# A fused attention and mixing kernel: casting loads gated by the third V block in place of the fourth, and another order of its 761 steps

## The chip, the cores and the metric

The kernel runs on one core of one Trainium2 chip. The metric is the device time of one execution in microseconds (us). A core has five engines that take their instructions from queues of their own and meet only at semaphores: PE (TensorE, matrix multiplication and transposes), DVE (VectorE), ACT (ScalarE, exponentials and sines), POOL (GpSimd, which also issues the DMAs that convert float32 to bfloat16) and SP (SyncE, which here issues all other DMAs). PEld in the profile is the loading of weights into PE, beside its matmuls.

## The reference

Four sequences of 768 positions go through an attention of 8 heads of 64 columns and then through a mixing layer. Heads 0, 2 and 6 are causal over all positions; the other five see the first 4 positions and a window of 64.

```python
scores = (1/8) * q @ k.T                      # per batch and head, 768 x 768
a = softmax(where(mask[head], scores, -1e9))
x = concat_heads(a @ v)                       # (4, 768, 512)
theta = x @ w_theta
zr, zi = x * cos(theta), x * sin(theta)
y = einsum('ts,bsd->btd', w_tok_r, zr) + einsum('ts,bsd->btd', w_tok_i, zi)
u = x + y
out = u + maximum(u @ w_ch, 0)                # float32
```

Inputs and output are float32; products are computed in bfloat16.

## The kernel before

**Tiles.** Each batch is cut into 6 blocks of 128 positions. The heads go in pairs, (0,2), (4,6), (1,3), (5,7), numbered 0 to 3. Scores are computed transposed and only where the mask leaves something: 17 units per batch, numbered 0 to 16. Units 0, 1, 2, 10, 11 and 12 belong to head pair 0; 3, 4, 5, 13 and 14 to pair 1; 6, 7 and 15 to pair 2; 8, 9 and 16 to pair 3. The eight PSUM banks are named in the steps, singly or as pairs starting at 0, 2, 4 and 6.

**Order.** Nothing is scheduled by a program. `ORDER` (line 57) is a list of 761 steps; the loop at line 535 runs them in turn, and each appends its instructions to the queue of its engine. A step is a name, its indices, a PSUM bank where it needs one, and at the end, for copies and elementwise products, the engine: A, D or P for ACT, DVE or POOL. Dependences become semaphore waits, so within one engine the list's order is the order of execution, and a waiting step holds all behind it on that engine.

**Steps.** In the order in which a batch b meets them:

- `k` constants (line 191): i the identity, a memsets on DVE, s four selects on POOL, b the masks' copies and negations on DVE, c other memsets. `kv` empties `vo` (line 215). `w.n` is n warm-up matmuls.
- `lf` (line 223): q and k of head pairs 0 and 1 of batch 0, as float32 on SP's queue, 384 KB each; `cf` (line 271) converts them on an engine. `lq` (line 228): the other q and k loads, converted by the DMA, on POOL's queue.
- `lv` (line 233): V in 6 blocks of 256 KB, float32, on SP's queue, into `st_v`. `cv` (line 388) converts a block into `vt`; `bv` copies part of it into `vo` for the window's previous block, `sv` the first four rows.
- `tq`, `eq` (lines 252, 267): transposes of q or k on PE and the copy out of PSUM (`ea`, `eb` in two parts). `ko` (line 276): the keys of the window's previous block with the first four.
- `pm`, `s`, `e`, `m`: in batch 0 masks are added in PSUM by `pm`; scores, exponentials, and in later batches a mask by DVE after the exponential.
- `av`, `n`: values of one block of rows and division by their sum, which gives x. `xp` with `xe` transposes x through PE (batch 0), `xd` by a DMA transpose on SP (line 421).
- `th`, `tr`, `z`: theta for two blocks, ACT's cosine and sine of it, and the products zr (part r) and zi (part i). `mx.b.t.p` (line 464): 4 matmuls of row block t with two of the six columns blocks of w_tok_r and w_tok_i; three such make y. `u` adds x. `ud` transposes u on SP, `up` with `ue` through PE. `ch`, `o`, `st`: product with w_ch, the final sum, the store. `ci`, `oi`, `si` are halves of these.
- `lw`, `lt`: the weights, converted by DMAs on POOL's queue; `wt`, `we` transpose w_tok through PE.

**Gates.** Two steps exist to hold loads back. `gw` (line 240) copies one element of a V block of batch 0 to a scrap tile on POOL, which therefore waits until that block has landed; the weights' loads `lw.t` and `lt` stand behind it on POOL's queue. `gv` (line 236) makes the V loads of batch 1 wait for a w_tok load.

```python
HOLD_V, HOLD_W = (5, 0), 3
...
    def hold_w():

        nc.gpsimd.tensor_copy(scrap, st_v[:1, HOLD_W, 0, :1])
```

Of the kernel before, what the change touches and what calls it, by code (L numbers as in the profile page):

```python
# [50 lines left out]
HOLD_V, HOLD_W = (5, 0), 3  # L51
# [6 lines left out]
k.i lf.q.0 k.a lf.k.0 lq.0.q.2 w.11.7 lf.q.1 kv.0.D lq.0.k.2 lf.k.1 k.s lv.0.0 w.11.7 lv.0.1 k.c cf.q.0.A lv.0.2 w.5.7 lq.0.q.3 k.b tq.0.q.0.0  # L58
lq.0.k.3 w.9.7 cf.k.0.A eq.0.q.0.0.A tq.0.k.0.1 pm.0.0.2 pm.0.12.4 ea.0.k.0.1.A pm.0.1.6 eb.0.k.0.1.A s.0.0.2 e.0.0.2 s.0.12.4 cf.q.1.P s.0.1.6
pm.0.2.0 lv.0.3 e.0.12.4 tq.0.q.2.2 e.0.1.6 cf.k.1.D s.0.10.4 tq.0.q.1.3 e.0.10.4 tq.0.k.1.6 eq.0.q.1.3.D s.0.2.0 eq.0.k.1.6.A eq.0.q.2.2.D s.0.11.4  # L60
lv.0.4 tq.0.k.2.3 e.0.2.0 ko.0.1.P pm.0.4.6 eq.0.k.2.3.D e.0.11.4 pm.0.3.0 cv.0.0.P s.0.4.6 s.0.3.0 bv.0.0.D e.0.4.6 s.0.14.2 ko.0.2.D pm.0.6.4
# [50 lines left out]
def kernel(ctx: ExitStack, tc: tile.TileContext, q, k, v, is_retrieval, n_sink, window, w_theta, w_tok_r, w_tok_i, w_ch, out):  # L112
    nc = tc.nc
# [119 lines left out]
    def load_v(b, j):  # L233
        nc.sync.dma_start(out=st_v[:, j], in_=v[b, :, j * 128:(j + 1) * 128].rearrange("h p d -> p h d"))
# [338 lines left out]
```

## Time and profile before

| | |
|---|---|
| median of 4 runs | 180.02 us (178.49 to 180.79) |
| the profiled execution | 179.5 us, of which 177.8 from its first to its last instruction |
| PE busy | 165.8 us (93%), 1793 matmuls in the record |
| PEld busy | 94.9 us (53%) |
| DVE busy | 138.5 us (78%) |
| ACT busy | 112.0 us (63%) |
| POOL busy | 54.7 us (31%) |
| granted PE clock | 1.00 |

The share of busy time is an average over stages. In a row of slices each digit is the busy share of a fortieth of the span in tenths. A timeline row has the start, the time that the instruction or run of instructions took, the engine (SPq is SP's queue of issues), the line, what is written and read, the count, and in brackets how long the engine stood idle before and what ended that. Matmuls overlap in their pipeline, so PE's busy time overstates its load; the distance from one start to the next is the better measure. The profile's own "x" counts miss a few matmuls; the weight loads, one ahead of each matmul, are complete, and times of PE steps are read from these.

### The profile page before, as it was taken

The numbers are of one execution on the slowest core, as the hardware profiler recorded it, in microseconds if no ns is written. First come the engines' busy times: TensorE is split into PE (matmuls) and PEld (weight loads), VectorE is DVE, ScalarE is ACT, GpSimd is POOL, SyncE is SP. The second block draws the span as 40 slices with busy tenths as digits, with TensorE's granted clock in tenths as the row PEclk, the third lists the DMA queues.
The fourth block names the chain that finished last, engine by engine and source line by source line (L and its number), as shares of the span: only waits on it lengthen the run. The fifth ranks groups of instructions, "written<-read, shape, count | busy, mean of one in ns | idle before, by whom it ended". The sixth has DMA issues, their size and how long they took to land.

```text
span 177.8 us, 4412 instructions
## 1 busy us (share of the span) xinstructions
PE 165.8 (93%) x1793; PEld 94.9 (53%) x1819; DVE 138.5 (78%) x268; ACT 112.0 (63%) x132; POOL 54.7 (31%) x86
## 2 busy tenths in 40 slices
PE   6868999999999998998999999999999999998992
PEld 6635578656654684543546864444445654443441
DVE  6347878898978977999869898979997928970483
ACT  3889999998999316798975408998761274300000
POOL 8414585686008800789160020040010000200000
PEclk9999999999999999999999999999999999999999
DMA  5997899999899999599999594957514548007856
GB/s 175 225 217 166 146 194 200 201 207 195 153 195 204 171 135 152 84 237 237 218 251 144 123 120 100 162 157 236 151 30 118 88 91 267 0 0 111 214 164 224
DMA packets 62372, 28.73 MB, mean 162 GB/s; under 512 B 48400, under 2 KB 59408, under 8 KB 62352
## 3 DMA queue, kind: packets, MB, share of 16 engines
q1 hardware_dynamic: 51952, 19.54, 53.9%
q0 software_dynamic: 10400, 8.92, 33.7%
q8 instruction: 14, 0.23, 0.6%
q14 instruction: 6, 0.05, 0.1%
HBM read 25.69 MB, written 6.29 MB: 180 GB/s over the span
## 4 chain that ended last, share of the span: by engine, by line
PE 70%; DMA 16%; DVE 7%; SPq 2%; issue 2%; POOL 0%; DVEq 0%
PE big L467 30%; PE big L450 9%; PE big L480 8%; PE big L323 8%; DMA st_v<-in_v_dram 7%; PE big L410 7%; DMA early<-early 4%; PE big L259 4%; DVE early L462 3%; DVE ot L483 2%; DMA uT<-u 2%; PE big L441 2%; DMA out_dram<-ot 2%; PE big L298 1%; SPq L226 1%
## 5 line engine op out<-in xcount | busy, mean ns | idle before, releaser
L353 ACT ACTIVATE P<-big 128x1024 bf16<-128x1024 f32 (+2 forms) x64 | 56.9, 947 | 11.3 <-PE big L323 11.1
L467 PE MATMUL big<-early,wtokTi 128*128 128x512 bf16 x71 | 26.9, 379 | 0.6 <-issue 0.5
L467 PE MATMUL big<-zi,wtokTi 128*128 128x512 bf16 x69 | 26.1, 379 | 0.6 <-issue 0.5
L467 PE MATMUL big<-early,wtokTr 128*128 128x512 bf16 x67 | 25.4, 380 | 0.1
L467 PE MATMUL big<-zr,wtokTr 128*128 128x512 bf16 x66 | 25.1, 380 | 0.3 <-DVE ot L483 0.2
L480 PE MATMUL big<-w_ch_sb,uT 128*128 128x512 bf16 (+1 forms) x96 | 23.7, 371 | 0.9 <-DMA uT<-u 0.7
L483 DVE SCALAR_TENSOR_TENSOR ot<-big,u 128x512 f32<-128x512 f32 (+1 forms) x25 | 16.3, 663 | 8.6 <-PE big L480 7.5
L467 PEld LDWEIGHTS <-wtokTr 128*128 128x128 bf16 x144 | 14.0, 98 | 16.5 <-issue 1.6
L467 PEld LDWEIGHTS <-wtokTi 128*128 128x128 bf16 x144 | 14.1, 98 | 14.1 <-issue 0.5
L323 PE MATMUL big<-qT,kT 64*128 64x128 bf16 (+3 forms) x240 | 19.4, 247 | 0.4 <-DVE ot L483 0.3
L410 PEld LDWEIGHTS <-P 128*128 128x128 bf16 x472 | 16.7, 97 | 3.8 <-DVE P L367 0.2
L410 PE MATMUL big<-vt,P 128*128 128x65 bf16 x372 | 17.2, 193 | 0.1
L454 ACT ACTIVATE ct<-big,half_pi 128x1024 f32<-128x1024 f32 x12 | 13.4, 1118 | 5.7 <-PE big L450 4.9
L375 DVE TENSOR_TENSOR P<-P,m_stream 128x1024 bf16<-128x1024 bf16 (+3 forms) x27 | 15.1, 569 | 2.2 <-ACT P L353 2.1
L480 PEld LDWEIGHTS <-uT 128*128 128x128 bf16 x100 | 9.1, 98 | 11.2 <-DMA uT<-u 1.4
L323 PEld LDWEIGHTS <-kT 64*128 64x128 bf16 x240 | 10.6, 94 | 7.4 <-issue 5.1
L265 POOL COPY kO<-kT 64x320 bf16<-64x320 bf16 (+3 forms) x10 | 4.4, 464 | 26.9 <-PE big L410 12.8
L462 POOL TENSOR_TENSOR early<-early,st 128x512 bf16<-128x512 bf16 x4 | 5.7, 1429 | 22.4 <-ACT st L455 22.4
L455 ACT ACTIVATE st<-big 128x1024 f32<-128x1024 f32 x12 | 12.3, 1022 | 0.0
L265 DVE COPY qT<-big 128x768 bf16<-128x768 bf16 x12 | 11.2, 948 | 1.0 <-PE big L259 1.0
L450 PE MATMUL big<-w_theta_sb,early 128*128 128x512 bf16 x45 | 10.9, 379 | 0.9 <-DMA early<-early 0.8
L263 ACT COPY kT<-big 128x768 bf16<-128x768 bf16 (+2 forms) x7 | 4.9, 713 | 10.5 <-PE big L259 9.3
(89 smaller groups left out, 286.4 us busy)
## 6 DMA issues: line engine op xcount, KB each, us to landing
st_v<-in_v_dram SPq DMA_DIRECT2D x24, 256.0 KB, 4.6
out_dram<-ot SPq DMA_DIRECT2D x23, 256.0 KB, 2.4
qb<-in_q_dram POOLq DMA_DIRECT2D x14, 192.0 KB, 6.8
kb<-in_k_dram POOLq DMA_DIRECT2D x14, 192.0 KB, 7.4
wtok<-in_moe_w_tok_r_dram POOLq DMA_DIRECT2D x6, 192.0 KB, 6.9
wtok<-in_moe_w_tok_i_dram POOLq DMA_DIRECT2D x6, 192.0 KB, 7.1
early<-in_q_dram SPq DMA_DIRECT2D x2, 384.0 KB, 5.4
early<-in_k_dram SPq DMA_DIRECT2D x2, 384.0 KB, 6.4
```

What stands on the lines that cost most here:

```text
L265: (nc.vector if eng == "D" else nc.gpsimd).tensor_copy(o, i)
L323: nc.tensor.matmul(*mms[g], start=not seeded, stop=True, skip_group_check=True)
L353: nc.scalar.activation(o, two(bank)[:, :, :o.shape[2]], AF.Exp, scale=scale)
L375: nc.vector.tensor_tensor(o, o, mk, ALU.mult)
L410: nc.tensor.matmul(o, l, r, start=(m == 0), stop=True, skip_group_check=True)
L450: nc.tensor.matmul(two(bank)[:, y], xT[b % 2][:, kk, i * 128:(i + 1) * 128], w_theta_sb[:, kk], start=(kk == 0), stop=(kk == KD - 1))
L454: nc.scalar.activation(ct[n], two(bank), AF.Sin, bias=half_pi)
L455: nc.scalar.activation(st[n], two(bank), AF.Sin)
L462: (nc.vector if eng == "D" else nc.gpsimd).tensor_tensor(z[b % 2][:, i], x[b % 2][:, i], s, ALU.mult)
L467: nc.tensor.matmul(one(bank), wtokT[n][:, s, t * 128:(t + 1) * 128], z[b % 2][:, s], start=(s == 0 and n == 0), stop=(s == NB - 1 and n == ...
L480: nc.tensor.matmul(one(bank)[:, d], uT[ui(b, t)][:, kk], w_ch_sb[:, kk, d], start=(kk == 0), stop=(kk == KD - 1))
L483: nc.vector.scalar_tensor_tensor(ot[(NB * b + t) % OT_BUFS][:, d], one(bank)[:, d], 0.0, u[ui(b, t)][:, d], ALU.max, ALU.add)
```

## The change

`HOLD_W` becomes 2, so that `gw` waits for the third V block of batch 0. `ORDER` is replaced by another list of the same 761 steps except for one: a warm-up of 9 matmuls has become one of 3. Banks, engines and places of steps differ throughout. `load_v` and `store` learn to issue from another engine's queue, which no step of the new list uses. The start of the list, old and new:

```diff
-HOLD_V, HOLD_W = (5, 0), 3
+HOLD_V, HOLD_W = (5, 0), 2
...
-k.i lf.q.0 k.a lf.k.0 lq.0.q.2 w.11.7 lf.q.1 kv.0.D lq.0.k.2 lf.k.1 k.s lv.0.0 w.11.7 lv.0.1 k.c cf.q.0.A lv.0.2 w.5.7 lq.0.q.3 k.b tq.0.q.0.0
-lq.0.k.3 w.9.7 cf.k.0.A eq.0.q.0.0.A tq.0.k.0.1 pm.0.0.2 pm.0.12.4 ea.0.k.0.1.A pm.0.1.6 eb.0.k.0.1.A s.0.0.2 e.0.0.2 s.0.12.4 cf.q.1.P s.0.1.6
-pm.0.2.0 lv.0.3 e.0.12.4 tq.0.q.2.2 e.0.1.6 cf.k.1.D s.0.10.4 tq.0.q.1.3 e.0.10.4 tq.0.k.1.6 eq.0.q.1.3.D s.0.2.0 eq.0.k.1.6.A eq.0.q.2.2.D s.0.11.4
-lv.0.4 tq.0.k.2.3 e.0.2.0 ko.0.1.P pm.0.4.6 eq.0.k.2.3.D e.0.11.4 pm.0.3.0 cv.0.0.P s.0.4.6 s.0.3.0 bv.0.0.D e.0.4.6 s.0.14.2 ko.0.2.D pm.0.6.4
-e.0.14.2 lv.0.5 tq.0.q.3.6 s.0.6.4 cv.0.1.P eq.0.q.3.6.D e.0.3.0 tq.0.k.3.7 pm.0.7.2 eq.0.k.3.7.D e.0.6.4 s.0.7.2 pm.0.8.0 ko.0.3.D e.0.7.2 pm.0.5.4
-sv.0.D s.0.8.0 gw.0 lw.t s.0.5.4 e.0.8.0 pm.0.15.6 pm.0.9.2 bv.0.1.D lt.0.0 cv.0.2.D s.0.15.6 e.0.5.4 bv.0.2.P av.0.0.0 e.0.15.6 s.0.9.2 n.0.0.0
-lt.0.1 av.0.1.4 e.0.9.2 lt.1.0 pm.0.16.6 n.0.1.4 pm.0.13.0 lt.1.1 cv.0.3.A s.0.16.6 s.0.13.0 lt.2.0 e.0.16.6 xp.0.0.2 xp.0.1.3 lt.2.1 xe.0.0.2.D
-av.0.2.4 bv.0.3.A xe.0.1.3.D lq.1.k.2 av.0.3.6 e.0.13.0 lq.1.q.0 cv.0.5.A n.0.3.6 th.0.0.2 lq.1.k.0 cv.0.4.A n.0.2.4 lq.1.q.2 bv.0.4.A lq.1.q.3
...
+k.i lf.q.0 k.a lf.k.0 w.11.7 lf.q.1 k.s lf.k.1 lv.0.0 w.11.7 lv.0.1 lq.0.q.2 cf.q.0.A k.b lv.0.2 w.5.7 kv.0.P tq.0.q.0.0 cf.k.0.D w.3.7 eq.0.q.0.0.A
+k.c tq.0.k.0.1 pm.0.0.2 lq.0.k.2 ea.0.k.0.1.A pm.0.12.4 eb.0.k.0.1.A s.0.10.6 lq.0.q.3 cf.q.1.D e.0.10.6 s.0.12.4 lq.0.k.3 pm.0.1.0 lv.0.3 s.0.0.2
+e.0.12.4 s.0.1.0 tq.0.q.1.6 cf.k.1.D e.0.1.0 pm.0.2.4 eq.0.q.1.6.D tq.0.k.1.7 e.0.0.2 s.0.2.4 s.0.11.0 eq.0.k.1.7.D tq.0.q.2.6 e.0.2.4 lv.0.4 pm.0.4.2
+eq.0.q.2.6.D ko.0.1.P e.0.11.0 pm.0.5.7 s.0.14.4 s.0.5.7 tq.0.k.2.6 cv.0.0.A s.0.4.2 e.0.14.4 eq.0.k.2.6.D pm.0.3.0 s.0.3.0 sv.0.D e.0.4.2 tq.0.q.3.6
+lv.0.5 pm.0.6.4 e.0.5.7 ko.0.2.P eq.0.q.3.6.D pm.0.7.2 e.0.3.0 cv.0.1.P bv.0.0.A tq.0.k.3.7 s.0.6.4 eq.0.k.3.7.D gw.0 s.0.7.2 lw.t e.0.6.4 pm.0.8.0
+lt.0.0 ko.0.3.D pm.0.9.6 e.0.7.2 cv.0.2.D s.0.8.0 bv.0.1.P pm.0.15.4 lt.0.1 e.0.8.0 s.0.9.6 s.0.15.4 lt.1.0 pm.0.16.2 e.0.15.4 av.0.0.0 lt.1.1
+s.0.16.2 n.0.0.0 lt.2.0 e.0.9.6 av.0.1.4 lt.2.1 bv.0.2.D pm.0.13.0 e.0.16.2 n.0.1.4 lq.1.q.2 av.0.2.6 cv.0.3.A lq.1.q.0 s.0.13.0 cv.0.5.D xp.0.0.2
+xp.0.1.3 lq.1.k.0 xe.0.0.2.A av.0.3.4 xe.0.1.3.D lq.1.k.2 e.0.13.0 th.0.0.2 n.0.3.4 lq.1.q.1 cv.0.4.A lq.1.k.3 n.0.2.6 bv.0.3.A bv.0.4.A lq.1.q.3
```

The hand-over from batch 0's mixing to batch 1's theta:

```diff
-m.1.16 mx.0.5.0.1 m.1.0 cv.1.4.D av.1.0.4 bv.1.0.P u.0.4.0 mx.0.3.1.2 cv.1.3.A lq.2.q.0 m.1.9 bv.1.2.A ch.0.1.0 bv.1.3.P n.1.0.4 bv.1.1.A bv.1.4.P
-av.1.1.6 xd.1.0 lq.2.k.1 av.1.2.4 n.1.1.6 mx.0.3.2.2 lq.2.k.2 o.0.1.0 xd.1.1 cv.1.5.A mx.0.5.1.1 n.1.2.4 av.1.3.6 av.1.5.4 n.1.3.6 mx.0.5.2.1 n.1.5.4
-xd.1.3 av.1.4.6 u.0.5.1 xd.1.2 tq.2.k.3.0 n.1.4.6 tq.2.q.1.1 eq.2.k.3.0.A tq.2.k.0.3 tq.2.q.2.4 xd.1.4 eq.2.k.0.3.D th.1.0.6 eq.2.q.2.4.D xd.1.5
...
-z.1.1.i.0.D lv.2.1 z.1.1.r.2.D s.2.7.4 ch.0.5.0 lv.2.2 z.1.1.i.1.P o.0.3.2 mx.1.0.0.3 o.0.0.1 e.2.7.4 o.0.5.0 z.1.2.i.1.P tq.2.q.3.2 s.2.6.6
...
+m.1.4 we.5.1.7.A we.3.1.6.D we.4.1.1.A s.1.6.4 s.1.8.2 m.1.12 s.1.16.6 e.1.6.4 m.1.1 mx.0.0.2.0 ud.0.1 m.1.3 e.1.16.6 mx.0.5.0.1 m.1.15 m.1.6 e.1.8.2
+lv.1.3 s.1.0.4 s.1.9.6 u.0.0.0 mx.0.5.1.1 cv.1.4.P lv.1.5 e.1.9.6 lq.2.k.0 cv.1.0.D mx.0.4.0.0 e.1.0.4 sv.1.D lq.2.k.2 lq.2.q.1 s.1.13.2 cv.1.1.A
+s.1.14.6 bv.1.0.D e.1.13.2 s.1.11.4 m.1.0 m.1.8 mx.0.4.1.0 e.1.14.6 m.1.5 m.1.9 av.1.1.2 bv.1.1.A mx.0.5.2.1 m.1.16 cv.1.2.A n.1.1.2 av.1.0.6 e.1.11.4
+bv.1.2.P mx.0.4.2.0 n.1.0.6 xd.1.1 av.1.2.2 u.0.5.1 mx.0.3.0.4 xd.1.0 n.1.2.2 cv.1.3.A bv.1.3.P av.1.3.6 xd.1.2 lq.2.q.0 s.1.10.2 n.1.3.6 tq.2.k.2.1
+lq.2.q.2 e.1.10.2 tq.2.k.0.5 m.1.13 lq.2.k.3 xd.1.3 mx.0.3.1.4 cv.1.5.A bv.1.4.P eq.2.k.2.1.A av.1.4.6 ud.0.0 eq.2.k.0.5.A th.1.0.2 ko.2.2.P n.1.4.6
+lq.2.k.1 u.0.4.0 xd.1.4 av.1.5.6 mx.0.3.2.4 n.1.5.6 tr.1.0.2 tq.2.q.0.5 u.0.3.4 xd.1.5 tq.2.q.2.0 tq.2.q.1.1 ud.0.3 eq.2.q.1.1.A tq.2.k.3.4
+z.1.0.i.0.P th.1.1.6 eq.2.k.3.4.D eq.2.q.2.0.A ud.0.2 lq.2.q.3 z.1.0.r.2.D ch.0.1.4 lv.2.3 tr.1.1.6 z.1.0.i.1.P eq.2.q.0.5.D ud.0.5 th.1.2.2 o.0.1.4
...
+mx.1.0.0.1 ud.0.4 o.0.5.0 e.2.0.4 s.2.4.2 z.1.1.i.1.D s.2.3.6 lv.2.5 mx.1.1.0.0 z.1.2.i.1.D e.2.3.6 m.2.2 mx.1.0.1.1 z.1.2.r.2.D e.2.4.2 st.0.3 st.0.0
```

The end of batch 2's mixing and the last blocks:

```diff
-st.2.1 th.3.2.6 z.3.0.i.0.D z.3.1.i.0.D mx.3.0.0.1 tr.3.2.6 z.3.1.r.2.D mx.3.1.0.3 z.3.1.i.1.D ch.2.5.4 o.2.3.0 z.3.2.i.0.P mx.3.1.1.3 mx.3.2.0.0
-z.3.2.i.1.D z.3.2.r.2.D mx.3.0.1.1 mx.3.2.1.0 o.2.5.4 mx.3.1.2.3 mx.3.0.2.1 u.3.1.3 u.2.4.2 mx.3.2.2.0 u.3.0.1 ud.2.4 mx.3.3.0.2 u.3.2.0 mx.3.5.0.1
-ud.3.0 mx.3.4.0.0 st.2.5 mx.3.3.1.2 st.2.3 ud.3.1 ch.2.4.3 mx.3.3.2.2 o.2.4.3 mx.3.4.1.0 st.2.4 u.3.3.2 ud.3.2 mx.3.5.1.1 mx.3.4.2.0 ud.3.3 ch.3.0.2
-u.3.4.0 mx.3.5.2.1 ud.3.4 o.3.0.2 ch.3.1.0 u.3.5.1 st.3.0 ch.3.3.2 o.3.1.0 ch.3.2.1 st.3.1 o.3.3.2 up.3.5.0 st.3.3 o.3.2.1 ch.3.4.2 ue.3.5.0.D st.3.2
-ci.3.5.0.3 o.3.4.2 ci.3.5.1.0 oi.3.5.0.3 st.3.4 oi.3.5.1.0 si.3.5.0 si.3.5.1
...
+o.1.5.2 ch.2.1.3 n.3.4.0 ud.2.2 mx.2.4.2.7 n.3.3.4 st.1.4 av.3.5.0 u.2.5.6 xd.3.3 th.3.0.4 n.3.5.0 xd.3.4 ch.2.0.2 xd.3.5 ch.2.2.6 o.2.0.2 st.1.5
+tr.3.0.4 u.2.4.7 th.3.1.0 ud.2.5 o.2.1.3 st.2.1 ch.2.3.7 z.3.0.i.1.D tr.3.1.0 z.3.0.r.2.D th.3.2.2 z.3.0.i.0.D z.3.1.i.1.P o.2.3.7 ch.2.5.0 tr.3.2.2
+st.2.3 mx.3.2.0.1 st.2.0 z.3.1.r.2.D ud.2.4 mx.3.0.0.7 z.3.1.i.0.D mx.3.1.0.2 o.2.2.6 z.3.2.r.2.D mx.3.2.1.1 st.2.2 mx.3.1.1.2 z.3.2.i.0.D mx.3.0.1.7
+z.3.2.i.1.D ch.2.4.3 mx.3.2.2.1 mx.3.0.2.7 u.3.2.1 o.2.4.3 mx.3.1.2.2 mx.3.3.0.1 u.3.1.2 u.3.0.7 mx.3.4.0.3 ud.3.0 mx.3.3.1.1 mx.3.5.0.2 st.2.4 ud.3.1
+mx.3.3.2.1 mx.3.4.1.3 u.3.3.1 o.2.5.0 mx.3.5.1.2 ud.3.3 mx.3.4.2.3 st.2.5 ch.3.1.0 ud.3.2 u.3.4.3 mx.3.5.2.2 o.3.1.0 ud.3.4 ch.3.0.1 u.3.5.2 st.3.1
+ch.3.3.0 o.3.0.1 up.3.5.2 st.3.0 ch.3.2.1 ue.3.5.2.D o.3.3.0 ci.3.5.1.2 o.3.2.1 st.3.3 ci.3.5.0.0 ch.3.4.3 st.3.2 oi.3.5.0.0 oi.3.5.1.2 si.3.5.0
+o.3.4.3 si.3.5.1 st.3.4
```

The two functions:

```diff
-    def load_v(b, j):
-        nc.sync.dma_start(out=st_v[:, j], in_=v[b, :, j * 128:(j + 1) * 128].rearrange("h p d -> p h d"))
+    def load_v(b, j, eng="S"):
+        (nc.scalar if eng == "A" else nc.sync).dma_start(out=st_v[:, j], in_=v[b, :, j * 128:(j + 1) * 128].rearrange("h p d -> p h d"))
...
-    def store(b, t, d=ALL):
-        nc.sync.dma_start(out=out[b, t * 128:(t + 1) * 128, d], in_=ot[(NB * b + t) % OT_BUFS][:, d])
+    def store(b, t, d=ALL, eng="S"):
+        (nc.gpsimd if eng == "P" else nc.sync).dma_start(out=out[b, t * 128:(t + 1) * 128, d], in_=ot[(NB * b + t) % OT_BUFS][:, d])
```

Steps of the early stage that change engine: `kv.0` from DVE to POOL; `cf.k.0` from ACT to DVE, `cf.q.1` from POOL to DVE; `cv.0.0` from POOL to ACT, `cv.0.5` from ACT to DVE; `bv.0.0` from DVE to ACT; `eq.0.k.1` from ACT to DVE; `ko.0.2` from DVE to POOL; `xe.0.0` and `xe.0.4` from DVE to ACT. On POOL the queue of the first 20 us reads, old and new:

```
k.i lq.0.q.2 lq.0.k.2 k.s lq.0.q.3 lq.0.k.3 cf.q.1 ko.0.1 cv.0.0 cv.0.1 gw.0 lw.t lt.0.0 bv.0.2 lt.0.1
k.i k.s lq.0.q.2 kv.0 lq.0.k.2 lq.0.q.3 lq.0.k.3 ko.0.1 ko.0.2 cv.0.1 gw.0 lw.t lt.0.0 bv.0.1 lt.0.1
```

## The prediction

> **What bounds the kernel now.** I read the page's slices first, then busy time by stage, then what waits and until when, then the chain of waits.
>
> The page, 40 slices of 4.4 us, busy tenths:
>
> ```profile
> PE   6868999999999998998999999999999999998992
> ACT  3889999998999316798975408998761274300000
> POOL 8414585686008800789160020040010000200000
> ```
>
> Stages of 10 us (columns: window, length, then busy us and instruction count of PE, PEld, DVE, ACT, POOL, then clock, DMA share, GB/s):
>
> ```profile
> 0.00:10.00 10.00, 7.01 (x66) 5.83 (x66) 4.25 (x14) 6.29 (x9) 5.92 (x15) 1.00 0.85 204
> 10.00:20.00 10.00, 8.66 (x123) 5.03 (x125) 7.22 (x12) 9.18 (x11) 3.25 (x8) 1.00 0.97 189
> ...
> 160.00:170.00 10.00, 9.43 (x44) 4.13 (x43) 3.33 (x6) 0.00 (x0) 0.00 (x0) 1.00 0.72 150
> 170.00:178.00 8.00, 4.28 (x26) 2.09 (x24) 4.14 (x8) 0.00 (x0) 0.00 (x0) 0.98 0.59 209
> ```
>
> PE is full from 20 us to 173 us. There a new order can gain only where PE has a hole. Adding up PE's steps at the pace of the chain (4 full matmuls 0.86, a transpose group 0.34, 30 ns a value matmul, 0.42 ns a score column) gives about 160 us of the 177.8. PE's start times run behind that running sum by 2.4 us at 8.4 us, 4.7 at 12.5, 6.3 at 20, 8.5 at 60, 9.7 at 71, 12 at 116, 13 at 150, 14.0 at the last matmul; 3.6 us follow it. Each rise is a hole. What makes the first ones, in order of time:
>
> ```profile
> 1.50 0.89 POOL L231 DMA_DIRECT2D qb<-in_q_dram  x1
> 2.84 14.67 SPq L234 DMA_DIRECT2D st_v<-in_v_dram  x6
> 8.22 2.64 ACT L353 ACTIVATE P<-big 128x1024 bf16<-128x1024 f32 x3
> 9.46 0.82 POOL L265 CAST qb<-early 128x768 bf16<-128x768 f32 x1 [3.13 <-DMA early<-in_q_dram]
> 11.47 0.56 DVE L265 CAST kb<-early 128x768 bf16<-128x768 f32 x1 [5.40 <-DMA early<-in_k_dram]
> 15.24 0.61 POOL L265 CAST vt<-st_v 128x512 bf16<-128x512 f32 x1 [1.16 <-DMA st_v<-in_v_dram]
> 18.84 0.18 POOL L242 COPY scrap<-st_v 1x1 f32<-1x1 f32 x1 [2.09 <-DMA st_v<-in_v_dram]
> 18.97 0.76 POOL L245 DMA_DIRECT2D w_theta_sb<-in_moe_w_theta_dram  x1
> ```
>
> First exp 8.22; lf.q.1 awaited to 9.4, lf.k.1 to 11.4, the first V block to 15.2; the gate (L242) opens at 18.8. Two later holes, from the chain of waits:
>
> ```profile
> 60.03 7.83 DMA early<-early
> ...
> 159.00 4.30 DMA uT<-u
> ```
>
> They hold PE 0.94 us at th.1.0 (67.9) and 1.01 us at ch.2.4 (163.3). One 0.52 stands before the last half blocks (ue.3.5), 0.36 before ch.0.5.
>
> [...]
>
> **The change, part by part.**
>
> *Start (−1.0).* k.s goes ahead of lq.0.q.2 on POOL. Its four selects take 1.84 us and need DVE's memset of 1.88, so they end near 3.5, not 4.95; then comes k.b (1.1 us), then cf.k.0, now on DVE, at the landing of lf.k.0 (5.09) for 0.56, beside cf.q.0 on ACT and not after it. With six warm-up matmuls fewer (0.6 us, which hid this) tq.0.k.0 starts near 5.9 instead of 6.47, and ea follows eq.0.q.0 (6.66) at once: first exp about 7.6, −0.6. POOL's first load is issued near 3.5, not 1.50; its packets, 3.7 us behind the issue in the trace, come 1 to 2 us later than 5.19. SP's queue moves 313 to 390 KB/us alone and 108 to 160 beside POOL's. So the 580 KB of lf left at 5.2 take about 2 us, not 6: lf.q.1 near 7.5, lf.k.1 near 8.5, V0 near 13 (11.5 to 15.2). lq.0.* shift little: they too had shared. kv.0 goes from DVE (1.68) to POOL: not shown; POOL's 128-column memset took 0.20, a one-column one 0.10, so some 1.7 us by length, 4 at worst. Behind it wait only three lq issues, and PE needs lq.0.k.2 near 13; taken at nothing.
> Four exps of head pair 0 now run first (s.0.10, 12, 0, 1), so ACT's gaps of 0.32 and 0.43 go. ACT loses eq.0.k.1 (0.7) to DVE and gains cv.0.0 (0.6), bv.0.0 (0.54), xe.0.0 (0.6). It reaches cv.0.0 near 12.5 and waits 0.6 for V0. Then e.0.9 ends near 21.6 (22.53 before), and th.0.0, whose xT now comes through ACT near 23.4, starts at 23.6 against 24.70. Ends: −1.6 with V0 there, +1.0 with V0 at 15.2.
>
> *Gate at V2, not V3.* V2 landed 1.09 us before V3 (17.70, 18.79). But POOL reaches gw.0 only behind ko.0.2 (new there, 1.25 us) and cv.0.1, near 16; with V2 at about 15.5 the gate no longer waits. First weight packets 1.5 us later, near 17.6, as V5 lands. The whole chain of casting loads comes 1.5 to 2 us earlier; PE hardly waited for it (wt.0.1 at 28.25, landed 27.72), so 0, but it lets the earlier th.0.0 pass.
>
> *Fewer switches to scores or transposes (−0.4).* On PE 31 instead of 34; each 0.30 more than the usual gap, 0.9 at most, about half hidden by a running matmul.
>
> *Batch 1 hand-over (−0.6).* Between av.1.0 and th.1.0 lie 5.8 us of PE work; normalising takes about 1.5 with DVE's queue, the DMA transpose 3.9 (median) or 7.8 (that one, beside lq.2 loads). Before, 7.1 us lay between av.1.1 and th.1.0 and PE still waited 0.94. Now lq.2.k.0, k.2, q.1 are issued ahead and the others held behind bv.1.2 and bv.1.3, so the transpose meets less. Past th.1.0 14 us of work precede mx.1.0.0 (10.4 before), cover for the phases of which more sit on POOL (1.2 to 1.8 us each). ud.0.2 moves far back on SP, behind xd.1.5 and ud.0.3 (1.2 us each), and lands about as ch.0.2 comes. Ends −1.3 and +1.5.
>
> *ch.2.4 (−1.0).* ud.2.4 waited for u.2.4, which stood on DVE behind u.3.1 (157.7). Now u.2.4 precedes the phases of batch 3; behind it on SP is st.2.2 with ud.3.0. The 1.01 goes; ends −1.0 and 0.
>
> *Batch 3 and tail (0).* From th.3.0 to the first mx.3 lie 8.6 us of PE work (9.3 before); the phases need about 8.1: 5.1 to tr.3.0's end as before, then 0.68, 1.22, 0.69 and an o. That just fits; next late would be mx.3.2.1. ue.3.5 now has ch.3.2 over it (−0.5), but the last block is a whole one: its o takes 0.69 for 0.42, its store 2.02 for 1.85 (+0.4).
>
> *Everything else (+1.0).* Some 40 copies and phases change engine and every score unit its place. I found no other wait, but an order that has not been profiled has some: 0 to +4, I take 1.0.
>
> Sum: −1.0 −0.4 −0.6 −1.0 +0.0 +1.0 = −2.0, against this execution's 179.5 (span 177.8 and 1.7 around it): 177.5. The median shown is 180.0, 0.5 above it; in its terms **177.9**.
>
> **Rivals.**
> *A. The waits only move.* V0 lands at 15.2 after all, as SP and POOL share the same engines; ACT stands at cv.0.0 for 2.7 us, with exps e.0.14 onward and PE's banks behind it. For it: all lq.0 loads precede V0 today (14.86). Start +1.0 in place of −1.0: 179.5, in median terms 179.9. Likewise if the later holes return elsewhere.
> [...]
> *C. The change does not do what it says:* the gate is open when POOL arrives and its number moves nothing. That is my forecast's view; it costs no time.
>
> **Chances.** Forecast 0.53 (own range 175.5 to 179.5), A 0.31, B 0.16. Within 1% of 180.0 (1.8 us, what a measurement of this kernel can tell) lie A and some of the forecast's upper end. Range 175.2 to 181.6: it takes in the forecast's ends and A, and leaves out most of B and a little below. Faster 0.50, same 0.33, slower 0.17.
>
> **What would show it.** First exp near 7.6; casts of lf.q.1 and lf.k.1 near 8 and 9; V0 near 13 and a wait under 1 us at ACT's first V cast; gate before 17 with no wait ahead of L242; V5 before 20; th.0.0 near 23.6; no PE hole at ch.2.4. I am wrong if V0 lands after 14.5, if DVE waits for V5, or if PE has holes over 1 us between 60 and 150.

## The result and the profile after

The changed kernel takes 180.19 us (median of 35 runs, 177.95 to 184.38), the kernel before 180.35 (56 runs): a ratio of 0.9991 with a 95% interval of 0.9966 to 1.0015, so no difference. The profiled execution took 178.72 us, 176.6 of them from first to last instruction; before it was 179.5 and 177.8. Some executions of these kernels are over 1.5% longer than the kernel's fastest, so all ratios, and the medians given with the experiments, are over the others alone (179.39 us for the changed kernel), and where an experiment's profile is of such a long one (1, 3, 7 and 9), at most its first 25 us are read.

The slices of the changed kernel, 40 of 4.4 us, busy tenths:

```profile
PE   6799999979999999999999999889999999999991
ACT  3699998968999596899885355858990038400000
POOL 7916837970024646080791142920051000100000
```

The same stages as before (window, length, then busy us and count of PE, PEld, DVE, ACT, POOL, then clock, DMA share, GB/s):

```profile
0.00:10.00 10.00, 7.24 (x72) 5.36 (x73) 5.24 (x15) 5.73 (x8) 7.72 (x17) 1.00 0.85 232
10.00:20.00 10.00, 9.44 (x132) 5.27 (x131) 7.33 (x10) 9.95 (x14) 5.73 (x13) 1.00 0.99 182
...
160.00:170.00 10.00, 9.95 (x49) 4.58 (x49) 5.03 (x8) 0.00 (x0) 0.00 (x0) 1.00 0.48 120
170.00:176.60 6.60, 2.84 (x21) 1.54 (x18) 3.07 (x6) 0.00 (x0) 0.00 (x0) 1.00 0.64 238
```

ACT is full from 10 to 20 us (9.95 for 9.18), PE has 9.44 for 8.66 there and 9.95 for 9.43 from 160 to 170 us. The price stands in the last column but three: POOL is busy 7.72 and 5.73 us in the first two stages, for 5.92 and 3.25. The timeline shows the forecast's early steps (start, length, engine, line, what is written and read, count, and in brackets the wait before):

```profile
2.85 12.98 SPq L234 DMA_DIRECT2D st_v<-in_v_dram  x6
3.51 0.89 POOL L231 DMA_DIRECT2D qb<-in_q_dram  x1
4.45 1.71 POOL L217 MEMSET vo<- 64x1950 bf16 x1
5.07 1.51 DVE L265 CAST kb<-early 128x768 bf16<-128x768 f32 x1 [0.99 <-DMA early<-in_k_dram]
7.22 0.70 DVE L265 CAST qb<-early 128x768 bf16<-128x768 f32 x1
8.04 4.96 ACT L353 ACTIVATE P<-big 128x1024 bf16<-128x1024 f32 x6
8.84 0.56 DVE L265 CAST kb<-early 128x768 bf16<-128x768 f32 x1 [0.92 <-DMA early<-in_k_dram]
12.84 0.66 ACT L263 CAST vt<-st_v 128x512 bf16<-128x512 f32 x1
15.95 0.18 POOL L242 COPY scrap<-st_v 1x1 f32<-1x1 f32 x1 [0.37 <-DMA st_v<-in_v_dram]
16.08 0.77 POOL L245 DMA_DIRECT2D w_theta_sb<-in_moe_w_theta_dram  x1
```

Casts of `lf.q.1` and `lf.k.1` at 7.2 and 8.8, a first V cast without a wait, a gate that waits 0.37 us in place of 2.09: the loads came as forecast or earlier. V0 landed at 10.78 (15.19), V5 at 18.81 (20.78), w_theta at 23.48 (24.70), and th.0.0 started at 23.83 (24.70). One line is out of place: `cf.k.0` took 1.51 us on DVE, where the same cast takes 0.56 four us later. Beside it POOL empties `vo`.

Where the gain went shows in the prediction's own measure, how far PE's starts lie behind the running sum of its work:

| At | before | after | difference |
|---|---|---|---|
| about 15 us | 5.0 | 4.1 | -0.9 |
| th.0.2, 31.5 us | 6.5 | 6.2 | -0.35 |
| first mx of batch 0, 36.7 us | 6.8 | 8.0 | +1.2 |
| ahead of batch 1's th.1.0, 62 us | 8.4 to 8.6 | 9.3 | +0.75 |
| behind it, 68 us | 9.7 | 9.4 | -0.25 |
| 81 us | 11.0 | 10.0 | -1.0 |
| 111 us | 11.8 | 11.1 | -0.65 |
| 115.9 us | 11.9 | 12.3 | +0.35 |
| 125 to 158 us | 13.0 | 13.0 | 0 |
| behind ch.2.4, 164.5 us | 13.65 | 13.0 | -0.7 |

Each hole that the forecast named closed. Two new ones opened, of 1.6 us at 36 and 1.0 us at 115. The timeline of the changed kernel at the first (z.0.1 is the phase product of the second pair of blocks; `wtokTr` is a copy `we`):

```profile
30.82 1.39 DVE L462 TENSOR_TENSOR zi<-x,st 128x512 bf16<-128x512 bf16 x1
32.14 3.63 DVE L462 TENSOR_TENSOR zr<-x,ct 128x1024 bf16<-128x1024 bf16 x2
33.48 1.20 POOL L462 TENSOR_TENSOR zi<-x,st 128x512 bf16<-128x512 bf16 x1
35.69 0.55 DVE L265 COPY wtokTr<-big 128x768 bf16<-128x768 bf16 x1
36.29 0.53 PE L259 MATMUL big<-ident,kb 128*64 128x128 bf16 x12 [1.39 <-DVE wtokTr L265]
36.76 0.82 PE L467 MATMUL big<-zr,wtokTr 128*128 128x512 bf16 x2
```

DVE's two zr products took 3.63 us: by single instructions the first lasted 1.21 and the second 2.50. In the kernel before the same two products, apart in time, took 1.22 and 1.23:

```profile
30.84 1.22 DVE L462 TENSOR_TENSOR zr<-x,ct 128x1024 bf16<-128x1024 bf16 x1
33.52 1.23 DVE L462 TENSOR_TENSOR zr<-x,ct 128x1024 bf16<-128x1024 bf16 x1
```

The long one began at 33.3 and waited for nothing; the chain of waits of the changed kernel puts that stretch down to no releaser:

```profile
32.21 1.62 DVE zr L462 x2
33.84 1.85 issue
35.69 0.56 DVE wtokTr L265
```

In the middle of it POOL does its half of the same phase, `z.0.1.i.0`, for 1.20 us. The DVE copy behind it frees the PSUM bank for which PE stands in `tq.1.k.2`. The second hole, same view:

```profile
110.73 1.16 POOL L462 TENSOR_TENSOR zi<-x,st 128x512 bf16<-128x512 bf16 x1 [3.76 <-ACT st L455]
110.79 1.39 DVE L265 CAST vt<-st_v 128x512 bf16<-128x512 f32 x1 [0.77 <-DMA st_v<-in_v_dram]
112.10 1.09 DVE L462 TENSOR_TENSOR zi<-x,st 128x512 bf16<-128x512 bf16 x1
112.59 2.05 POOL L265 COPY kO<-kT 128x320 bf16<-128x320 bf16 x2
113.11 1.46 DVE L462 TENSOR_TENSOR zr<-x,ct 128x1024 bf16<-128x1024 bf16 x1
114.50 1.27 DVE L473 TENSOR_TENSOR u<-early,big 128x512 bf16<-128x512 bf16 x2
115.22 1.02 PE L480 MATMUL big<-w_ch_sb,uT 128*128 128x512 bf16 x4 [0.97 <-DVE u L473]
```

The V cast `cv.3.5` waits 0.77 us for its block and then takes 1.39 beside POOL's product, where others take 0.42; `z.2.1.i.0` and `z.2.1.r.2` take 1.09 and 1.46 for 0.68 and 1.22; the `ko` on POOL takes 2.05, elsewhere 0.59. Behind them stands `u.1.5`, whose bank ch.1.2 needs. Summed over the DVE casts and phase products that took over 0.1 us more than is usual for their kind, the excess is 2.7 us before and 6.1 us after. Not all of it costs time: two more stretched products of the changed kernel, at 69.7 us (2.22) and 150.5 us (1.59), opened no hole on PE.

### The profile page after: what moved, and what is told of

Its sections match the earlier page's. It is cut to its first block, busy times and chain, and to the rows that moved or that the text cites. A ratio compares the mean times of both kernels' runs of the same rounds, so it can differ in the third digit from the quotient of the medians.

```text
span 176.6 us, 4403 instructions
## 1 busy us (share of the span) xinstructions
PE 165.1 (93%) x1788; PEld 94.3 (53%) x1813; DVE 136.2 (77%) x255; ACT 114.1 (65%) x136; POOL 62.3 (35%) x95
## 4 chain that ended last, share of the span: by engine, by line
PE 67%; DVE 10%; DMA 7%; ACT 7%; SPq 3%; issue 3%; DVEq 0%
PE big L467 31%; PE big L480 9%; PE big L410 8%; PE big L450 7%; ACT P L353 6%; PE big L323 6%; PE big L259 4%; DMA uT<-u 3%; SPq L234 3%; DMA early<-in_k_dram 2%; DVE early L462 2%; DMA st_v<-in_v_dram 2%; DVE zr L462 2%; PE big L441 1%; DVE zi L462 1%
## 5 line engine op out<-in xcount | busy, mean ns | idle before, releaser
L467 PE MATMUL big<-early,wtokTr 128*128 128x512 bf16 x70 | 26.6, 380 | 0.2
L467 PE MATMUL big<-early,wtokTi 128*128 128x512 bf16 x69 | 26.1, 379 | 0.2 <-issue 0.2
L467 PE MATMUL big<-zi,wtokTi 128*128 128x512 bf16 x67 | 25.4, 379 | 0.5 <-issue 0.3
L480 PE MATMUL big<-w_ch_sb,uT 128*128 128x512 bf16 (+1 forms) x98 | 23.8, 371 | 1.2 <-DVE u L473 1.0
L410 PEld LDWEIGHTS <-P 128*128 128x128 bf16 x472 | 17.2, 97 | 4.7 <-issue 0.4
L454 ACT ACT_TABLE_LOAD x4 | 5.1, 1283 | 14.9 <-PE big L450 11.9
L265 POOL COPY vo<-vt 64x384 bf16<-64x384 bf16 x9 | 7.4, 834 | 18.7 <-DVE vt L265 14.3
L473 DVE TENSOR_TENSOR u<-early,big 128x512 bf16<-128x512 bf16 x12 | 7.9, 683 | 7.6 <-PE big L467 7.6
L231 POOL DMA_DIRECT2D kb<-in_k_dram x14 | 10.2, 731 | 6.1 <-DVE kO L265 4.0
```

The costliest lines, as they stand in the source:

```text
L231: nc.gpsimd.dma_start(out=t[:, 2 * n:2 * n + 2], in_=a[b, h0:h1 + 1:2].rearrange("h (p j) d -> p h (j d)", p=128))
L410: nc.tensor.matmul(o, l, r, start=(m == 0), stop=True, skip_group_check=True)
L454: nc.scalar.activation(ct[n], two(bank), AF.Sin, bias=half_pi)
L467: nc.tensor.matmul(one(bank), wtokT[n][:, s, t * 128:(t + 1) * 128], z[b % 2][:, s], start=(s == 0 and n == 0), stop=(s == NB - 1 and n == ...
L480: nc.tensor.matmul(one(bank)[:, d], uT[ui(b, t)][:, kk], w_ch_sb[:, kk, d], start=(kk == 0), stop=(kk == KD - 1))
```

## The experiments

Theory 1: an elementwise step on POOL and one on DVE hold each other up when both run, and the new order lays more of them side by side; the gate's number moves nothing. Theory 2: DVE is simply full, or other waits take what is won. Each ratio is to the kernel before. All lie within 2% of 1, so what counts is whether an interval leaves out 1, and the changed kernel's own 0.9966 to 1.0015.

**1. The gate's number undone.**

```diff
-HOLD_V, HOLD_W = (5, 0), 2
+HOLD_V, HOLD_W = (5, 0), 3
```

> The changed kernel with the gate put back to the fourth V block (the number alone). Theory 1 (the number moves nothing, because PE hardly waits for the casting loads): in the changed kernel the gate step ran at 15.95 us with V2 landing at 15.90 and V3 at 16.82, so it now runs near 16.9 and w_theta lands about 0.9 us later, near 24.4 instead of 23.48; th.0.0 (23.83) may move by up to 0.6 us, the total by less than 0.5 us: ratio to the kernel before 0.996 to 1.003. Theory 2 (the early gate is what costs, by crossing with V4 and V5): V4 and V5 land at least 0.3 us earlier than 17.92 and 18.81 and the total falls by 1 us or more, ratio under 0.994.

Ratio 1.0017 (0.9979 to 1.0054), median 179.44. The gate opened at 17.43 for 15.95. V4 and V5 landed 0.5 us later, not earlier, so Theory 2 is out; w_theta landed at 23.10 for 23.48, where I had expected it later, and th.0.0 started at 23.89 for 23.83: opening the gate 1.5 us earlier moved th.0.0 by 0.06.

**2. One phase half of POOL moved behind a weight load's issue.**

```diff
-... tr.0.2.6 z.0.1.i.0.P tq.1.q.2.4 we.2.0.1.D ... lt.5.0 mx.0.2.0.2 ...
+... tr.0.2.6 tq.1.q.2.4 we.2.0.1.D ... lt.5.0 z.0.1.i.0.P mx.0.2.0.2 ...
```

> The changed kernel with one POOL step, the product z.0.1.i.0, moved behind the issue of lt.5.0 on POOL's queue. Theory 1 (POOL's two-input product holds DVE's for its own length: z.0.1.r.2 took 2.50 us beside it and 1.21 to 1.22 elsewhere, so we.2.0.1 freed its PSUM bank late and PE stood 1.6 us in tq.1.k.2): z.0.1.r.2 takes about 1.22 us, we.2.0.1 ends near 35.0 instead of 36.24, mx.0.1.0 starts near 35.5 instead of 36.74, the total falls by 0.6 to 1.2 us, ratio about 0.994. Theory 2 (DVE was slowed by DMA traffic or by something that stays): z.0.1.r.2 keeps 2 us or more and the total does not move. Theory 3 (the hole goes but PE waits for ACT's cosines or the tq.1 copies next): mx.0.1.0 comes 1 us earlier and the total stays within 0.3 us.

Ratio 0.9876 (0.9798 to 0.9953), median 177.60, but over 3 executions only. The timeline of this kernel at the same place:

```profile
32.28 2.35 DVE L462 TENSOR_TENSOR zr<-x,ct 128x1024 bf16<-128x1024 bf16 x2
34.74 0.56 DVE L265 COPY wtokTr<-big 128x768 bf16<-128x768 bf16 x1
35.49 2.30 POOL L462 TENSOR_TENSOR zi<-x,st 128x512 bf16<-128x512 bf16 x2
35.60 0.50 PE L259 MATMUL big<-ident,kb 128*64 128x128 bf16 x12
36.03 0.82 PE L467 MATMUL big<-zr,wtokTr 128*128 128x512 bf16 x2
```

With POOL away the two products take 2.35 us together, not 3.63, and PE's wait is gone. That is Theory 1. POOL's two halves now lie from 35.5 to 37.8 beside copies out of PSUM, which keep their usual 0.55; DVE's next product out of SBUF, `z.0.2.i.0`, took 1.26 for 0.68.

**3. `kv.0` given back to DVE.**

```diff
-k.i lf.q.0 k.a lf.k.0 ... w.5.7 kv.0.P tq.0.q.0.0 ...
+k.i lf.q.0 k.a kv.0.D lf.k.0 ... w.5.7 tq.0.q.0.0 ...
```

> The changed kernel with the emptying of vo (three memsets) back on DVE, ahead of k.b. Theory 1 (POOL's memset of 2.56 us held DVE's cast of lf.k.0, which took 1.51 us instead of 0.56): that cast takes 0.55 to 0.6 us, the first exp starts near 7.5 instead of 8.04; lq.0.k.2 is issued near 4.4 instead of 6.84 and all lq.0 loads land earlier, which removes PE's 0.21 and 0.42 us waits for them; V0 lands a little later than 10.78, up to 12.5. th.0.0 comes up to 0.5 us earlier, the total falls by 0.2 to 0.5 us, ratio 0.997. Theory 2 (the cast was long for another reason): it keeps 1.5 us, and the first exp stays at 8.0.

Ratio 0.9932 (0.9896 to 0.9969), median 178.53. `cf.k.0` took 0.70 for 1.51. The first exp came at 8.29, which looks no earlier than 8.04. But PE's early matmuls ran at half their pace in this execution (last section), and only executions of like pace compare. Two executions at that pace with `kv.0` on POOL had the first exp at 8.68 and 8.67 (experiments 2 and 5); at the full pace it came at 8.04 with `kv.0` on POOL (the changed kernel) and at 7.65 with it on DVE (experiment 12). So `kv.0` on POOL costs the first exp some 0.39 us at either pace. V0 landed at 11.31, w_theta at 24.70, and th.0.0 started at 24.29, so the gain doesn't show there. The kernel is faster than the one before; against the changed kernel the two intervals just touch. Where the rest of the gain arises this profile doesn't show.

**4. The selects moved ahead in the kernel before.**

```diff
-k.i lf.q.0 k.a lf.k.0 lq.0.q.2 w.11.7 lf.q.1 kv.0.D lq.0.k.2 lf.k.1 k.s lv.0.0 ...
+k.i lf.q.0 k.a lf.k.0 k.s lq.0.q.2 w.11.7 lf.q.1 kv.0.D lq.0.k.2 lf.k.1 lv.0.0 ...
```

> The kernel before with only the four selects of k.s moved ahead of POOL's first two loads. Theory 1 (what brought lf and V early in the changed kernel is that POOL's first packets come about 2 us later): lf.q.1 lands near 7.2 instead of 9.32, lf.k.1 near 8.8 instead of 11.45, V0 between 10.5 and 13 instead of 15.19; POOL's lq.0.q.2 still lands near 10.3 to 11, so PE's first wait stays and the wait for lf.k.1 (0.68 us) goes; the total falls by 0.3 to 0.8 us, ratio about 0.997. Theory 2 (the earlier landings come from kv.0 standing between POOL's loads): lf.q.1 and V0 stay within 1 us of where they were, the total does not move.

Ratio 1.0046 (1.0013 to 1.0079): slightly slower, where I had expected a gain. The loads moved as in the change (`lf.q.1` 8.13, `lf.k.1` 9.25, V0 12.07), which is Theory 1's mechanism. But in this execution `lf.k.0` landed at 6.56 for 5.09 and PE had the slow early pace of experiment 3, the first exp came at 9.94, and PE then waited 1.1 us for `lq.0.q.2`, which the old order transposes third and which now landed at 11.75. Early V by itself thus didn't help the old order. That it helps one that first works on head pairs 0 and 1, as the change does, is likely and wasn't tried by itself.

**5. The three POOL phase halves of batch 0 on DVE.**

```diff
-z.0.0.i.1.P ... z.0.1.i.0.P ... z.0.2.i.1.P
+z.0.0.i.1.D ... z.0.1.i.0.D ... z.0.2.i.1.D
```

> The changed kernel with the three phase halves of batch 0 that POOL does (z.0.0.i.1, z.0.1.i.0, z.0.2.i.1) done by VectorE, at the same places of the order. Theory 1 (an elementwise step of POOL stretches the one of VectorE beside it, and the other way round): although VectorE gets three halves of 0.68 us more, z.0.1.r.2 takes 1.2 us instead of 2.50, z.0.0.i.0 0.68 instead of 1.39, and the hole before mx.0.1.0 is under 0.6 us instead of 1.6; time 178.5 to 179.8, ratio to the kernel before 0.990 to 0.997. Theory 2 (VectorE is simply full there, and a step that takes 2.5 us waits for something of its own): z.0.1.r.2 stays at 2 us or more, or VectorE is later by the 2.0 us that it gets, and mx.0.1.0 comes 1 us later still; time 180.5 to 181.5.

Ratio 0.9922 (0.9882 to 0.9962), median 178.28. The timeline of this kernel:

```profile
31.45 0.68 DVE L462 TENSOR_TENSOR zi<-x,st 128x512 bf16<-128x512 bf16 x1
32.05 2.35 DVE L462 TENSOR_TENSOR zr<-x,ct 128x1024 bf16<-128x1024 bf16 x2
34.32 0.69 DVE L462 TENSOR_TENSOR zi<-x,st 128x512 bf16<-128x512 bf16 x1
34.92 0.55 DVE L265 COPY wtokTr<-big 128x768 bf16<-128x768 bf16 x1
```

DVE does two products more before its copy (one of them ahead of these lines) and still reaches it 0.77 us earlier (34.92 for 35.69), although this execution came to th.0.0 0.6 us later. That decides against Theory 2: DVE was held, not full. PE kept those 0.77 us until 61 us; then th.1.0 waited 0.60 for a transpose of x, and 0.1 was left.

**6. The second hole as well: `cv.3.5` behind `u.1.3.3`.** To the edit of experiment 2 comes

```diff
-z.2.0.i.0.D cv.3.5.D z.2.1.i.0.D ... u.1.5.0 mx.2.0.0.2 u.1.3.3 cv.3.2.P ...
+z.2.0.i.0.D z.2.1.i.0.D ... u.1.5.0 mx.2.0.0.2 u.1.3.3 cv.3.5.D cv.3.2.P ...
```

> The changed kernel with two steps moved: z.0.1.i.0 of POOL behind lt.5.0 (as in the second run), and the V cast cv.3.5 of VectorE from ahead of z.2.1.i.0 to behind u.1.3.3, so that VectorE doesn't wait there for a V block that landed at 110.7. Theory 1: mx.0.1.0 has no hole of over 0.6 us, u.1.5.0 ends 1 to 1.5 us earlier relative to the matrix work, ch.1.2.0 doesn't wait for its bank, and the two losses of 1.6 and 1.0 us that the changed kernel showed are gone: 177.5 to 178.8, ratio 0.983 to 0.993. Theory 2 (other steps take up the time): ratio 0.995 to 1.003.

Ratio 0.9926 (0.9888 to 0.9964), median 178.55. The timeline:

```profile
111.41 0.69 DVE L462 TENSOR_TENSOR zi<-x,st 128x512 bf16<-128x512 bf16 x1 [0.67 <-ACT st L455]
112.02 2.19 DVE L462 TENSOR_TENSOR zr<-x,ct 128x1024 bf16<-128x1024 bf16 x1
114.13 1.27 DVE L473 TENSOR_TENSOR u<-early,big 128x512 bf16<-128x512 bf16 x2
115.09 1.04 PE L480 MATMUL big<-w_ch_sb,uT 128*128 128x512 bf16 x4
```

PE has no wait ahead of ch.1.2 any more, and from 112 to 116 us it won 0.85 us on the changed kernel, although POOL's product still stretches `z.2.1.r.2` to 2.19. What opened this hole is thus `cv.3.5` in its old place, waiting and stretched. It hangs on when the V block lands: in experiment 2's execution, which lacks this edit, the block was there, the cast took 0.43 us without a wait, and ch.1.2 didn't wait either. In time the edit shows nothing on top of experiment 2's (0.9876). Both holes are closed in this execution, but th.1.0 stood 1.71 us between them for its transposed x and took the first gain back. This is the third loss:

```profile
64.58 1.90 PE L450 MATMUL big<-w_theta_sb,early 128*128 128x512 bf16 x8 [1.59 <-DMA early<-early]
```

**7. The same with `kv.0` on DVE.**

> The run before with kv.0 given back to VectorE right behind k.a as well. Theory 1: casts of K at 0.7 us instead of 1.5, but the first loads of the batch land up to 0.6 us later behind kv.0, the start as in the third run; together with both losses gone 177 to 178.5, ratio 0.980 to 0.990, the fastest of all. Theory 2: no better than the changed kernel with kv.0 alone moved, ratio 0.992 to 0.997.

Ratio 0.9922 (0.9896 to 0.9947), median 178.67: no better than without it.

**8. The gate's number alone, in the kernel before.**

```diff
-HOLD_V, HOLD_W = (5, 0), 3
+HOLD_V, HOLD_W = (5, 0), 2
```

> The kernel before with the gate's number alone changed, third V block in place of the fourth. Theory 1 (the number moves nothing, since the block it names and the gate's own place on POOL end within 1 us of each other): gate and w_theta earlier by 0 to 0.9 us, th.0.0 by under 0.3; 179.6 to 180.8, ratio 0.997 to 1.002. Rival: the casting loads collide with the last V blocks, V5 lands 1 us or more later, ratio 1.004 to 1.015.

Ratio 1.0006 (0.9977 to 1.0036). The gate opened 1.41 us earlier (17.43), beyond my range; V5 landed at 20.57 for 20.78, so V wasn't hurt, but w_theta landed later, at 25.48 for 24.70, and th.0.0 started at 25.88 for 24.70. The time didn't follow: with 1 the number moves nothing, in either order.

**9. Theory 3: the arrival of transposed x is a wait of its own.**

```diff
-... eq.2.k.0.5.A th.1.0.2 ko.2.2.P n.1.4.6 lq.2.k.1 u.0.4.0 xd.1.4 av.1.5.6 mx.0.3.2.4 n.1.5.6 ...
+... eq.2.k.0.5.A ko.2.2.P n.1.4.6 lq.2.k.1 u.0.4.0 xd.1.4 av.1.5.6 mx.0.3.2.4 th.1.0.2 n.1.5.6 ...
```

> The changed kernel with one step moved: th.1.0 of the matrix engine (the phase product of batch 1, whose tr follows by itself) from ahead of av.1.5.6 to behind mx.0.3.2.4, so 1.7 us of matrix work that needs no transposed x stands ahead of it. Profiled runs of the changed order had th.1.0 wait 0 to 4.0 us for xd.1.0, a transpose by DMA that is in flight beside three casting loads of batch 2. Theory 3 (that arrival is a wait of its own that takes back what is won before it, and its scatter is in the medians): th.1.0 starts without a wait or with one shorter by 1.6 us; the median is 179.2 to 179.8, ratio 0.993 to 0.998. Theory 2 (no such loss in the runs without a profile; th.1.0 and tr.1.0 are only later): 180.0 to 181.0, ratio 0.999 to 1.005.

Ratio 0.9943 (0.9915 to 0.9971), median 178.86. One step moved brings about 0.5%, in a kernel whose own profiled execution shows no wait at th.1.0; the interval overlaps the changed kernel's by a hair, so this is likely and not certain. The profiled executions of 2, 5 and 6 had that wait at 0.35, 0.60 and 1.71 us: there xd.1.0 landed 4.8, 5.0 and 6.1 us after its issue, in the changed kernel's profile after 4.0. The likeliest reading is that other executions of the changed kernel have the wait too, and that its profile drew a good one; no run shows that directly.

**10. All three.** The edits of 5, of 6's diff and of 9.

> The three phase halves of batch 0 on VectorE, cv.3.5 behind u.1.3.3, and th.1.0 behind mx.0.3.2.4, in the changed kernel. Theory 1 with 3: each of the three losses is worth its own size in a profiled run (0.8, 0.8 and 0 to 1.7 us), since the next one no longer takes it back: 177.0 to 178.2, ratio 0.980 to 0.988, and the interval lies below those of the fifth and sixth runs' 0.992. Theory 2 (a further wait takes it back): ratio 0.990 to 0.996.

Ratio 0.9870 (0.9813 to 0.9928), median 177.88 (5 executions). Below 5 and 6, but the intervals overlap. Its timeline has no wait ahead of th.1.0, and a new one ahead of ch.1.2:

```profile
65.74 1.89 PE L450 MATMUL big<-w_theta_sb,early 128*128 128x512 bf16 x8
115.09 1.04 PE L480 MATMUL big<-w_ch_sb,uT 128*128 128x512 bf16 x4 [0.81 <-DMA uT<-u]
```

DVE was done with `u.1.5` in time, but the transpose ud.1.2 that ch.1.2 also needs landed 6.2 us after its issue, for 4.8 in the changed kernel. Of the second loss only some 0.1 us was saved here, which is Theory 2's outcome for that part; in experiment 12 the same wait is 0.81 again.

**11. All three and `kv.0` on DVE.**

> The run before with kv.0 on VectorE right behind k.a as well. If the third run's gain (ratio 0.993) comes from the start, it adds to the others: 176.2 to 177.6, ratio 0.974 to 0.985. If it came by what it moved later (the wait for xd.1.0), it adds nothing: ratio within 0.002 of the run before.

Ratio 0.9854 (0.9783 to 0.9924), median 177.79 (6 executions): the lowest ratio, ahead of both kernels, and not told apart from 10. Twice (7 and 11) `kv.0` added nothing that shows to the other edits. Alone it gave 0.7% on the kernel before, some 1.2 us, of which 0.39 are seen at the first exp; the rest stays open.

**12. Is the transpose late because of the casting loads beside it?**

```diff
-... bv.1.3.P ... lq.2.q.2 e.1.10.2 tq.2.k.0.5 m.1.13 lq.2.k.3 ... ko.2.2.P n.1.4.6 lq.2.k.1 ...
+... bv.1.3.P ... e.1.10.2 tq.2.k.0.5 m.1.13 ... ko.2.2.P lq.2.q.2 lq.2.k.3 n.1.4.6 lq.2.k.1 ...
```

> The run before with two casting loads of batch 2 (lq.2.q.2 and lq.2.k.3) moved on POOL's queue from behind bv.1.3 to behind ko.2.2, so they are issued some 3.5 us later, when xd.1.0 and xd.1.1 should have landed. Theory 3 in its strong form (xd.1.0 is late because of the casting loads in flight beside it): xd.1.0 lands under 64 us and within 5 us of its issue, where profiled runs of the other orders had 63.4 to 67.6, and th.1.0 doesn't wait; tq.2.q.2 then waits up to 1 us for its load; time 176.2 to 177.8, ratio 0.976 to 0.986. Rival (the transposes are slow by themselves, whatever the loads do): xd.1.0 lands 6 us or more after its issue as in the eleventh run, and the two loads are late on top: 178.3 to 179.5, ratio 0.988 to 0.995.

The mechanism in the main, the time no: ratio 1.0003 (0.9968 to 1.0037), median 179.91. xd.1.0 landed 5.0 us after its issue (57.67 to 62.68), in experiment 11 7.7 us (58.76 to 66.45). That alone proves little, since with the three loads beside it xd.1.0 also took 4.0 to 6.1 us in other executions. The two behind it are clearer: xd.1.2 took 3.8 us and xd.1.3 3.1, where the changed kernel and experiments 2, 5, 6, 10 and 11 had 5.3 to 7.4 and 4.7 to 6.9. Then the loads were late. The timeline:

```profile
64.99 1.89 PE L450 MATMUL big<-w_theta_sb,early 128*128 128x512 bf16 x8
66.81 1.27 PE L259 MATMUL big<-ident,qb 128*64 128x128 bf16 x36
70.03 0.53 PE L259 MATMUL big<-ident,kb 128*64 128x128 bf16 x12 [1.95 <-DMA kb<-in_k_dram]
```

`lq.2.k.3` landed 6.6 us after its issue, where I had allowed tq up to 1 us of wait. From mx.0.3.2 to ch.0.2 PE lost 1.5 us on experiment 11. In these two executions, which of transposes and loads goes first only chose which of the two PE waited for.

## Why the prediction was wrong

**Right: the loads.** `lf.q.1` and `lf.k.1` landed at 7.2 and 8.8 (forecast 7.5 and 8.5), V0 at 10.78, earlier than my 13 and than the range that I gave it. The gate came before 17, after 0.37 us of wait where I had none; e.0.9 ended near 21.6 (21.57), and th.0.0 started near 23.6 (23.83). Rival B, the slower outcome with 0.16, didn't come: V5 landed at 18.81, before 20, and from 17 to 18 us the trace of the changed kernel has 912 packets on SP's queue and 3 on POOL's, so V and the weights hardly met there. Rival A's 179.9 is what came in time, not by V0, on which A rested, but as its last clause has it: "if the later holes return elsewhere". Rival C's statement, that the gate's number moves nothing, held (experiments 1 and 8).

**Right: the holes that go.** The waits at th.1.0 and ch.2.4 went in the profiled execution (1.0 and 0.7 us by the table; I had priced the second at 1.0), no phase of batch 3 was late, and from 68 to 81 us PE won 0.7 more than I had forecast.

**Wrong, the step that decided: "Everything else (+1.0)", with "I found no other wait".** By the table everything else cost +2.1 us in the profiled execution: +1.6 at 36 us, +1.0 at 115, -0.5 between 37 and 62 and about 0 in the rest. The cause of the first is shown by experiments 2 and 5. The second goes back to `cv.3.5` (experiment 6): part a wait for a V block (0.77 us), part the stretch of it and of the two steps behind it (1.6 us); no run takes these apart, and no ratio shows what closing this hole is worth. My own sign looked for holes between 60 and 150 us, and the larger one came at 36.

I had counted the phases "of which more sit on POOL (1.2 to 1.8 us each)" as cover, a price that POOL alone pays. In truth DVE pays too. The trace shows it: 1.28 us of excess on `z.0.1.r.2` beside a POOL product of 1.20, and copies out of PSUM beside the next such product unharmed at 0.54. It shows in the ends as well: each of the changed kernel's four stretched zr products (2.50, 2.22, 1.46 and 1.59 us) ended 1.08 or 1.09 us after a POOL step beside it had ended, little less than its usual 1.22. So in these four DVE did next to nothing while that step ran. Engines thus don't meet at semaphores only: `z.0.1.r.2` waited for none. By the records it starts first (33.27, POOL's product 33.48) and is yet the one held, while in the kernel before, at 77.7 us, a zr product on DVE and a product on POOL start 0.01 us apart, and POOL's is held (2.23 for 1.16) and DVE's not (1.21). So their starts don't tell which is held, and no run shows what does.

**Wrong: `kv.0` on POOL "taken at nothing".** I priced it at 1.7 us of POOL and looked only at what queues behind it on POOL. Its three memsets took 2.56 us and held `cf.k.0` for 0.95 of its 1.51. First exp 8.04, forecast 7.6; most of the difference is the 0.39 us of experiment 3. Of the start's forecast -1.0 the table has -0.9 at 15 us and -0.35 at 31.5; most of what went was lost between 20.6 and 21.7 us, and I have not traced it further.

**Wrong: the start and the hand-over of batch 1 held only in some executions.** Seven profiled executions run the changed kernel's order up to th.0.0: its own and those of experiments 1, 2, 5, 6, 9 and 10. Three reached th.0.0 at 23.8 to 23.9 us, four at 24.3 to 24.7, and 24.7 is where the kernel before had it. In two of the late ones PE's early pace was the slow one; for the others I have no cause. In the hand-over, "the transpose meets less" fits the profiled execution (xd.1.0 landed 4.0 us after its issue, 7.8 in the kernel before). But the order starts the transposes right beside three casting loads, and experiment 9's 0.5% suggests that they are late in others. Both would explain why the profiled execution is 0.8 us faster than before's and the median isn't, where I had put both medians at one distance of 0.5. That is argued, not shown.

The sum against the profiled execution: start -0.35, everything else +2.1, hand-over and what follows to 81 us -1.7, ch.2.4 -0.7, tail -0.5, so -1.2 of the span; forecast -2.0. Switches (-0.4) can't be told apart in it: in both traces the weight loader idles 0.12 us between two mx matmuls and 0.42 from one to scores or q/k transposes, which gives the 0.30 that I took for each, but no run shows how much of it a running matmul hides. So 0.8 of the 2 us by which the time missed are seen in this pair of executions, and the rest is put down to the scatter just named. (The forecast's own sum, 177.5 and 0.5, gives 178.0 and not 177.9.)

## What to carry to other kernels

Before moving an elementwise step to an idle POOL, look at what DVE does in those microseconds: beside a DVE product or cast from SBUF it held DVE for up to its whole length here (1.28 us beside a product of 1.20), beside a copy out of PSUM it cost nothing (0.54 us, alone 0.55). In a trace, a step that takes twice the time of its likes and waits for nothing (here 2.50 us for 1.22) may be held by a neighbour; compare single durations with the shortest of the kind, and its end with the neighbour's end. And where a hole depends on a DMA that is in flight beside others, one profiled execution doesn't tell its usual size (xd.1.0 took 4.0 to 6.1 us in four profiled ones): give PE work ahead of it, and look at the median.

## What the runs showed of the hardware

A POOL product of 128x512 (1.16 to 1.20 us) stretched a DVE product of 1.22 to 2.50 and one of 0.68 to 1.39; POOL memsets stretched a DVE cast of 0.56 to 1.51. It goes the other way too: beside DVE's products `ko` on POOL took 2.05 for 0.59, and a product on POOL 2.23 for 1.16 (77.7 us of the kernel before). One pair shows both: at 113 us of the changed kernel DVE's product took 1.46 for 1.22, and the second part of `ko` on POOL, usually 0.19 us, took 1.19 and ended at 114.64, just after DVE's (114.58). In the first 9 us PE's pace changes within an execution, and not at the same time in all: 128-column matmuls followed each other after 0.11 us up to 7.0 us in the kernel before and up to 5.8 in the changed kernel, and after 0.06 from 7.1 and 6.6 on; in experiment 11 it was 0.11 where experiment 12, with the same steps up to there, had 0.06, and the first exp came at 8.28 and 7.65. The profile gives a granted clock of 1.00 for the stretches on both sides of the change (0 to 5 and 7 to 9 us before, 0 to 5 and 6 to 9 after); what sets the pace wasn't tried.
